# A decode-attention kernel: softmax maximum and values block one set sooner, the fifth key unit in halves, and the TensorE loop laid out afresh

## The chip, the cores and the metric

The kernel runs on one core of one Trainium2 chip. The metric is device time in microseconds (us), of which each kernel was run several times. "Span" is the time from the first to the last instruction in a profiled execution; it is about 2 us below the timed figure.

In the profile before, TensorE does the matrix work (9791 matmuls), VectorE (DVE in the profile, 1079 instructions) and ScalarE (ACT, 655) copy and do the softmax, SyncE (SP) issues 88 of the 91 transfers, and 16 DMA engines move the data.

## The reference, cut to what matters

One token is decoded. The work that counts is attention over a cache: 8 key/value heads, 65536 positions of 256 numbers each, in bf16, so 268 MB of keys and as much of values. 16 query heads share them, two per key/value head. Projections and a small gated MLP come on top.

```python
q = (x @ wq).reshape(B, Sq, Hq, Dh)...            # one token, 16 heads of 256
scores = jnp.einsum("bhqd,bhkd->bhqk", q, k) * (Dh ** -0.5)
p = _softmax(scores, axis=-1)
o = jnp.einsum("bhqk,bhkd->bhqd", p, v)
... @ wo                                           # plus the residual and the MLP
```

Every byte of the cache is used once. The whole kernel moves 549 MB.

## The kernel before: the parts that matter

Keys come in 32 units (k0, k1, ...) of 8 MB, 4 units to a head, and so do values (v0, v1, ...). There are three slots of 8 MB in on-chip memory: slots 0 and 1 alternate between key units, and slot 2 takes values. SyncE issues the transfers in one fixed order, and each issue waits until its slot is free:

```python
    def k_item(u):                       # key unit u goes into slot u % 2
        need = [("FREE", u - 2)] if u >= 2 else ()
        if 2 <= u < U:                   # U = 4: k2 and k3 in halves
            need = {0: [("FREEH", u - 2)], 1: need}
        slot_item("k", u, u % 2, [... two halves ...] if u < U else None, need)

    def v_item(t):                       # value unit t goes into slot 2
        slot_item("v", t, 2, None, [("VFREE", t - 1)] if t else [...])

    for u in range(U - 1): k_item(u)     # k0 k1 k2, all in halves
    v_item(0)
    k_item(U - 1); k_item(U); k_item(U + 1)          # k3 (halves), k4, k5
    for t in range(1, NT):               # v1 k6 v2 k7 ...
        v_item(t)
        if t + U + 1 < NU: k_item(t + U + 1)
```

TensorE goes through one key unit per turn, in 8 sets. A set transposes 16 positions per partition, multiplies them with the query (QK) and lays the scores out (JT). From turn 4 on, a turn also has a values block: unit v(t) is multiplied with the softmax weights in turn t + 4, since the maximum of a whole head (4 key units) is needed first. That maximum takes two small matmuls (M1T and BC) with VectorE work between, and every fourth turn ScalarE then takes the exponentials.

```python
    def turn_K(u):
        ...
        at = {(3, 0): ghostly(lambda: pe_m1t(...)), (4, 0): ghostly(lambda: pe_bc(...)),
              (SETS - 1, 0): ghostly(lambda: pe_oT(v))}     # (set, step): softmax matmuls
        k_sets(u, range(0, CSETS + 1), at)       # sets 0..4 (CSETS = 4)
        bar()                                    # the loop's code is cut into parts here
        ghostly(block)()                         # values block: 64 matmuls of 512 columns
        bar()
        k_sets(u, range(CSETS + 1, SETS), at)    # sets 5..7
```

The end of the block releases slot 2 (VFREE), half of the unit releases half of a key slot (FREEH), and the end of the turn releases all of it (FREE). In the first four turns the block is jumped over; `ghostly` marks what is left out there.

TensorE's instructions are one hardware loop over turns. Even and odd turns have their own code for the sets, as they read different slots, and share the block. In memory the order is: odd first part, even first part, block, odd second part, even second part. Turn 0 is an even one.

```python
   with eng.If_ne(parity, 0):  turn(... odd ...)
   with eng.If_eq(parity, 0):  turn(... even ...)
```

## Time and profile before

| | before |
|---|---|
| time, median of the first 3 runs | 1286.32 us (1285.24 to 1288.13) |
| span of the profiled execution | 1284.3 us |
| moved | 549 MB, 427 GB/s over the span |
| DMA queue, share of 16 engines | 99.2% |
| TensorE busy | 986.9 us (77%) |

From the page of the kernel before: the busy time of each engine, then rows of the picture in 40 slices (each about 32 us; a digit is a tenth), and the summary of the chain that ended last.

```profile
PE 986.9 (77%) x9791; PEld 660.5 (51%) x9791; DVE 576.1 (45%) x1079; ACT 436.1 (34%) x655; POOL 8.0 (1%) x38
...
DMA  9999899999999999999999999999999999999998
GB/s 405 412 432 438 339 443 425 425 447 433 427 429 449 429 425 447 431 429 425 449 433 425 431 447 429 425 447 433 427 425 451 431 425 435 443 429 425 411 449 354
...
DMA 65%; PE 24%; ACT 6%; issue 3%; SPq 2%; DVE 0%; ACTq 0%; DVEq 0%
```

The DMA engines are the busy ones. One slice alone stands out before the very end: the fifth, near 128 to 160 us, with 339 GB/s. The windows view of the same trace puts the stretch with the gap beside the steady part, and then looks into the gap (a packet counts in the window in which it starts, so shares over 1 are possible; PEclk is the granted clock of TensorE, 1.00 is full):

```profile
core 0: us, PE busy (x) PEld busy (x) DVE busy (x) ACT busy (x) POOL busy (x), PEclk, DMA share, GB/s
127.00:176.00 49.00, 41.85 (x430) 29.58 (x430) 27.30 (x53) 22.53 (x36) 0.00 (x0) 0.93 0.87 369
176.00:1182.00 1006.00, 787.94 (x7794) 532.60 (x7786) 461.71 (x861) 350.72 (x526) 0.00 (x0) 0.87 1.00 434
...
144.00:148.00 4.00, 3.60 (x38) 2.62 (x35) 2.68 (x6) 2.15 (x4) 0.00 (x0) 1.00 0.91 393
148.00:152.00 4.00, 2.20 (x36) 1.04 (x36) 0.69 (x2) 2.65 (x8) 0.00 (x0) 1.00 0.00 0
152.00:156.00 4.00, 4.00 (x55) 2.21 (x55) 1.11 (x3) 0.62 (x3) 0.00 (x0) 1.00 0.74 262
```

From 148 to 152 us no packet starts. What happens there is in the timeline (start, duration, engine, line, operation; in brackets the idle time before it and what ended it; "issue" there means that the profile shows nothing that it waited for). First TensorE in turns 0 and 4, then SyncE's issues of k5 and v1:

```profile
47.53 1.44 PE L411 MATMUL ps_t<-ident_f,ring 128*128 128x128 f32 x6 [6.56 <-issue]
...
130.50 1.97 PE L411 MATMUL ps_t<-ident_f,ring 128*128 128x128 f32 x8 [3.79 <-DMA ring<-in_A_k_cache_dram]
...
149.80 1.90 PE L411 MATMUL ps_o<-ring,p_sb 128*4 128x512 bf16 x32 [2.02 <-ACT p_sb L572]
151.63 0.61 PE L411 MATMUL ps_m<-rowsum,ones_f 128*128 128x2 f32 x4
152.17 1.90 PE L411 MATMUL ps_o<-ring,p_sb 128*4 128x512 bf16 x32
```

```profile
126.65 0.33 SPq L882 DMA_DIRECT2D ring<-in_A_k_cache_dram  x1
154.11 0.33 SPq L882 DMA_DIRECT2D ring<-in_A_v_cache_dram  x1
```

The view of the chain that ended last (start, duration, what) has k4 from its issue to its landing:

```profile
103.83 26.62 DMA ring<-in_A_k_cache_dram
```

Read the timeline from the bottom. v1 is issued at 154.11 us, as soon as the values block of turn 4 is done with v0. The transfer ahead of it, k5, landed at 150.63 (the landing times in this document are the completions of the semaphores in the trace). So the queue stood empty. The block was late because turn 4 began only at 130.50, when the whole of k4 had landed, though TensorE was free from 126.70. And k4, one transfer of 8 MB, was issued late because all of k2 had to be read first.

After that there is no gap of this kind. From 176 to 1202 us a unit lands every 19.35 us, 8.39 MB / 19.35 us = 434 GB/s. TensorE waits in nearly every turn, as the waits view of the whole execution says (who waited for whom: us in total, times, longest):

```profile
PE ps_t L411 <- DMA ring<-in_A_k_cache_dram: 136.5, 28, 6.5
PE ps_o L411 <- DMA ring<-in_A_v_cache_dram: 82.3, 26, 13.2
```

### The profile page before, as it was taken

What the parts mean: (1) busy time and instruction counts of PE and PEld (TensorE: products, weight loads), DVE (VectorE), ACT (ScalarE), POOL (GpSimd) and SP (SyncE); (2) the same over time, 40 slices, a digit from 0 to 9 for tenths busy, and PEclk for the clock granted to TensorE, in tenths of its full rate; (3) what the DMA queues carried; (4) which work ended last, traced back from release to release, by engine and by line L of the source; (5) the groups of instructions that cost most, each with busy time, mean ns of one, the idle gap of its engine ahead of it and who ended that gap; (6) DMA issues with size and microseconds to landing.
All of it is one profiled execution on the core that took longest, in us unless ns stands there. A gap on an engine that the chain in (4) does not pass through costs nothing.

```text
span 1284.3 us, 23619 instructions
## 1 busy us (share of the span) xinstructions
PE 986.9 (77%) x9791; PEld 660.5 (51%) x9791; DVE 576.1 (45%) x1079; ACT 436.1 (34%) x655; POOL 8.0 (1%) x38
## 2 busy tenths in 40 slices
PE   4799888787688777787886797687788778786573
PEld 3576565555455555454554465454455545554321
DVE  4476464444444443453543454443444543444210
ACT  1355443333333433333333243333433333332200
POOL 2000000000000000000000000000000000000000
PEclk9899898878988887897888888878988887998787
DMA  9999899999999999999999999999999999999998
GB/s 405 412 432 438 339 443 425 425 447 433 427 429 449 429 425 447 431 429 425 449 433 425 431 447 429 425 447 433 427 425 451 431 425 435 443 429 425 411 449 354
DMA packets 13444, 549.20 MB, mean 428 GB/s; under 512 B 1398, under 2 KB 3448, under 8 KB 4088
## 3 DMA queue, kind: packets, MB, share of 16 engines
q1 hardware_dynamic: 13426, 549.03, 99.2%
q8 instruction: 8, 0.13, 0.0%
q14 instruction: 4, 0.03, 0.0%
q10 hardware_dynamic: 6, 0.00, 0.0%
HBM read 549.03 MB, written 0.00 MB: 427 GB/s over the span
## 4 chain that ended last, share of the span: by engine, by line
DMA 65%; PE 24%; ACT 6%; issue 3%; SPq 2%; DVE 0%; ACTq 0%; DVEq 0%
DMA ring<-in_A_v_cache_dram 44%; DMA ring<-in_A_k_cache_dram 21%; PE ps_t L411 9%; PE ps_o L411 9%; ACT kt_all L481 5%; PE ps_q L411 4%; SPq L882 2%; PE ps_m L411 2%; DMA ring<-in_A_wo_dram 1%; ACT S_sb L562 1%; ACT p_sb L572 0%; DVE kt_all L479 0%; DVE kt_all L698 0%; ACTq L984 0%; PE ps_s L411 0%
## 5 line engine op out<-in xcount | busy, mean ns | idle before, releaser
L411 PE MATMUL ps_t<-ident_f,ring 128*128 128x128 f32 x4096 | 620.5, 296 | 167.4 <-DMA ring<-in_A_k_cache_dram 136.5
L479 DVE COPY kt_all<-ps_t 128x1024 bf16<-128x1024 bf16 x768 | 486.9, 684 | 401.4 <-PE ps_q L411 393.3
L411 PEld LDWEIGHTS ps_t<-ident_f,ring 128*128 128x128 f32 x4096 | 481.1, 150 | 330.4 <-issue 160.6
L481 ACT ACTIVATE kt_all<-ps_t 128x1024 bf16<-128x1024 bf16 x256 | 261.9, 1023 | 571.3 <-PE ps_q L411 571.2
L411 PE MATMUL ps_o<-ring,p_sb 128*4 128x512 bf16 x2044 | 160.6, 469 | 97.2 <-DMA ring<-in_A_v_cache_dram 82.3
L411 PE MATMUL ps_q<-kt_all,q_cur 128*2 128x512 bf16 x2056 | 172.6, 414 | 0.7 <-DVE kt_all L479 0.6
L503 ACT ACTIVATE s<-ps_q 98x512 bf16<-98x512 f32 x257 | 151.6, 590 | 1.3 <-PE ps_q L411 1.3
L411 PEld LDWEIGHTS ps_o<-ring,p_sb 128*4 128x4 bf16 x2044 | 50.5, 95 | 171.4 <-issue 120.7
L572 ACT ACTIVATE p_sb<-S_sb 128x128 bf16<-128x128 bf16 x64 | 18.9, 307 | 173.4 <-PE ps_o L411 173.1
L587 DVE RECIPROCAL rs<-ps_m 128x4 f32<-128x4 f32 x29 | 5.3, 182 | 148.1 <-PE ps_m L411 148.1
L411 PEld LDWEIGHTS ps_s<-sel_bf,s 128*128 128x128 bf16 x1032 | 65.0, 98 | 5.4 <-ACT s L503 1.9
L411 PE MATMUL ps_s<-sel_bf,s 128*128 128x8 bf16 x1032 | 63.7, 167 | 1.3 <-ACT s L503 1.3
L630 DVE CAST ob_sb<-ps_o 100x512 bf16<-100x512 f32 x29 | 20.1, 691 | 97.6 <-PE ps_o L411 97.6
L411 PEld LDWEIGHTS ps_q<-kt_all,q_cur 128*2 128x2 bf16 x2056 | 26.6, 79 | 49.0 <-issue 49.0
L411 PEld LDWEIGHTS ps_m<-rowsum,ones_f 128*128 128x128 f32 x116 | 18.8, 231 | 18.1 <-issue 18.1
L481 ACT ACT_TABLE_LOAD x7 | 9.0, 1283 | 50.7 <-PE ps_q L411 50.7
L411 PE MATMUL ps_m<-rowsum,ones_f 128*128 128x2 f32 x116 | 21.3, 288 | 0.0
L532 DVE TENSOR_REDUCE m1p<-S_sb (+1 forms) x33 | 13.9, 422 | 4.4
L411 PE MATMUL ps_q<-ring,oT_h 128*1 128x448 bf16 x28 | 8.1, 467 | 9.8 <-DMA ring<-in_A_wo_dram 9.8
L530 DVE CAST S_sb<-ps_s 128x256 f32 (+1 forms) x33 | 13.6, 413 | 1.9 <-PE ps_s L411 1.9
L562 ACT ACTIVATE S_sb<-S_sb,negmax 128x512 bf16<-128x512 bf16 x16 | 13.2, 850 | 3.0 <-DVE negmax L556 3.0
L411 PE MATMUL ps_m<-diag,ones_f 2*128 2x2 f32 x58 | 11.0, 256 | 0.6 <-DVE diag L547 0.6
(94 smaller groups left out, 134.0 us busy)
## 6 DMA issues: line engine op xcount, KB each, us to landing
ring<-in_A_k_cache_dram SPq DMA_DIRECT2D x8, 4096.0 KB, 30.4
ring<-in_A_v_cache_dram SPq DMA_DIRECT2D x1, 4096.0 KB, 28.1
ring<-in_A_wq_dram SPq DMA_DIRECT2D x1, 3584.0 KB, 11.8
ring<-in_A_wo_dram SPq DMA_DIRECT2D x7, 448.0 KB, 22.6
ring<-in_A_v_cache_dram SPq DMA_DIRECT2D x1, 2048.0 KB, 32.6
ring<-in_B_w_gate_dram SPq DMA_DIRECT2D x1, 1568.0 KB, 15.5
ring<-in_B_w_up_dram SPq DMA_DIRECT2D x1, 1568.0 KB, 18.9
ring<-in_B_w_down_dram SPq DMA_DIRECT2D x2, 784.0 KB, 21.6
```

The source lines that it names most:

```text
L411: return pe.matmul(*a, **k)
L479: O(e, ("EV", s, m), lambda it: nc.vector.tensor_copy(out=kt[:, :], in_=tb[:, :]), f"ev{m}")
L481: O(e, ("EV", s, m), lambda it: nc.scalar.activation(out=kt[:, :], in_=tb[:, :], func=ACTF.Copy), f"ev{m}")
L503: O("act", ("EVQ", s), lambda it: nc.scalar.activation(out=s2[s % 2][0:QROWS, :], in_=ps_q[0:QROWS, :], func=ACTF.Copy), "evq")
L530: O("dve", ("SCOPY", u), lambda it: nc.vector.tensor_copy(out=S_sb[:, at(it, SBN), :], in_=ps_sn), "sc")
L532: O("dve", ("SMAX", u), lambda it: nc.vector.tensor_reduce(out=m1p[:, :, at(it, 1)], in_=S_sb[:, at(it, SBN), :].rearrange("p n i -> p i n ...
L562: O("act", ("EXP", h, i), lambda it, i=i: nc.scalar.activation(out=S_sb[:, :, i], in_=S_sb[:, :, i], func=ACTF.Exp, bias=negmax[:, i:i + 1 ...
L572: O("act", ("PC", t, c), lambda it: nc.scalar.activation(out=p_sb[:, c, :, :], in_=S_sb[:, n:n + CH, :], func=ACTF.Copy), "pc")
L587: O("dve", ("RS", t), lambda it: nc.vector.reciprocal(out=rs[:, :, :], in_=ps_m[0:P, C_TOT:C_TOT + NH * rep]))
L630: O("dve", ("OB", t), lambda it: nc.vector.tensor_copy(out=ob_sb[0:OROWS, :], in_=ps_o[0:OROWS, :]))
L882: eng.dma_start(fn[0], fn[1]).then_inc(sems[sem], 16)
```

## The change

It has three parts. The fifth key unit, k4, is taken in halves like the first four, so its first half may be issued when half of k2 has been read. The values block moves from after set 4 to after set 3 of each turn, and the two softmax matmuls that come before it move with it. And the code of the even turn's second part comes right after the block, so turn 0, which jumps over the block, comes out right there.

```diff
@@ sizes
+    UH = U + 1
@@ k_item
-        if 2 <= u < U:
+        if 2 <= u < UH:
             need = {0: [("FREEH", u - 2)], 1: need}
-        slot_item("k", u, u % 2, [...halves...] if u < U else None, need)
+        slot_item("k", u, u % 2, [...halves...] if u < UH else None, need)
@@ k_sets (which load a set waits for)
-                W_item("pe", ... ("k", min(u, U - 2 + u % 2), 1))
+                W_item("pe", ... ("k", min(u, UH - 1 - (UH - 1 - u) % 2), 1))
@@ turn_K
-        at = {(3, 0): ghostly(lambda: pe_m1t(v + U - 1)), (4, 0): ghostly(lambda: pe_bc(v + U - 1)),
+        at = {(2, 2): ghostly(lambda: pe_m1t(v + U - 1)), (3, 0): ghostly(lambda: pe_bc(v + U - 1)),
-        k_sets(u, range(0, CSETS + 1), at)
+        k_sets(u, range(0, CSETS), at)
         ... values block ...
-        k_sets(u, range(CSETS + 1, SETS), at)
+        k_sets(u, range(CSETS, SETS), at)
@@ the loop's code (k counts its parts: 0 first sets, 2 second sets)
-                        with eng.If_ne(parity, 0): ... odd turn ...
-                        with eng.If_eq(parity, 0): ... even turn ...
+                        for odd in (1, 0) if k == 0 else (0, 1):
+                            if odd:
+                                with eng.If_ne(parity, 0): ... odd turn ...
+                            else:
+                                with eng.If_eq(parity, 0): ... even turn ...
```

The number of matmuls and the bytes moved are the same.

More of the change, by code (lines that the diff above doesn't have):

```diff
@@ L270, in k_item @@
         need = [("FREE", u - 2)] if u >= 2 else ()
-        if 2 <= u < U:
+        if 2 <= u < UH:
             need = {0: [("FREEH", u - 2)], 1: need}
-        slot_item("k", u, u % 2, [("slot%d" % (u % 2), CH), ("half%d" % (u % 2), CH)] if u < U else None, need)
+        slot_item("k", u, u % 2, [("slot%d" % (u % 2), CH), ("half%d" % (u % 2), CH)] if u < UH else None, need)
     def v_item(t):
@@ L727, in k_sets @@
             if q % CSETS == 0:
-                W_item("pe", ("k", u, 0) if q == 0 else ("k", min(u, U - 2 + u % 2), 1))
+                W_item("pe", ("k", u, 0) if q == 0 else ("k", min(u, UH - 1 - (UH - 1 - u) % 2), 1))
             s = u * SETS + q
@@ L1026, in loop @@
                             continue
-                        with eng.If_ne(parity, 0):
-                            turn(it, it, b0, b1, False)
-                            if k == len(cuts[0]) - 1:
-                                step_regs(("iter",))
-                        with eng.If_eq(parity, 0):
-                            turn(it, it, a0, a1, False)
+                        for odd in (1, 0) if k == 0 else (0, 1):
+                            if odd:
+                                with eng.If_ne(parity, 0):
+                                    turn(it, it, b0, b1, False)
+                                    if k == len(cuts[0]) - 1:
+                                        step_regs(("iter",))
+                            else:
+                                with eng.If_eq(parity, 0):
+                                    turn(it, it, a0, a1, False)
                     step_regs(("turn",))
```

## The prediction

> **What bounds the kernel now.** The transfers. The page shows the 16 DMA engines 90% busy or more in nearly every slice: 549 MB at 427 GB/s over 1284.3 us. From 176 us on, the chain of waits runs through DMA with TensorE pieces only between. By the landing times in the trace, from 176 to 1202 us an 8 MB unit lands every 19.35 us, each issued 13 us or more before the one ahead of it landed; the windows view gives 176 to 1182 us a DMA share of 1.00. There a sooner TensorE cannot help.

> The one hole is at the start: over 127 to 176 us the DMA share is 0.87, 369 GB/s. Unit k4 is issued at 103.83 us (release of unit 2) and lands at 130.45; TensorE stands from 126.65 to 130.50 for it, then restarts at half clock (eight transposes take 1.97 us, not 1.09). The first values block ends at 154.1, where v1 is issued. But k5 landed at 150.63. So v1 lands 25.28 us after k5 instead of 19.35, and k5 itself 20.18 after k4: lost 5.93 + 0.83 = 6.76 us.

> **What the change does there.**
> 1. k4 in halves: its first half is issued when half of unit 2 is read (about 92 us), and lands about 120.8. Turn 4 starts straight on, 3.85 us sooner and without the half-clock restart (its first set took about 2.5 us longer than the usual 2.85): v1 about 6.4 us sooner.
> 2. The values block one set sooner: another 2.9 us.
> 3. Loop layout: turn 0 stalls 6.56 + 1.27 us ("issue") at the jump to its second part, then runs at half clock; about 8 us can go, but turn 3 then waits for k3 (landing near 100.4), so perhaps 2 us reach turn 4. [...] five 16 KiB instruction packets between 20 and 52 us (one at 45.04, inside the stall), none again until 1210 us. So the gain comes once.

> v1 would be issued at about 143 to 145 us, some 5 us before k5 lands at about 149.8. An issue on an idle queue costs about 2.4 us (v1: 21.81 us from issue to landing), so the hole closes entirely, and everything later shifts with it. The parts overlap; each alone I estimate at about 6, 2.9 and below 1 us, capped at the 6.76 us hole. The softmax chain in fewer sets may cost TensorE about 1 us a turn; it waits 3 us for v there anyway.

> **Prediction.** 1286.32 - 6.8 = 1279.5 us; range 1278.0 to 1281.8. Faster by over 2%: 0.01; within 2%: 0.985; slower: 0.005.

> **In the profile:** DMA share 1.00 from k4's landing to v1's; v1 landing near 169 us, not 175.9; the 6.56 us stall in turn 0 gone; no wait for k4 at about 126 us; TensorE waiting longer for v (about 6 us a turn, not 3) and less for k in the steady turns, the 19.35 us rhythm unchanged.

> **What would make it wrong:** transfers pacing below 19.35 us per unit with earlier issue; a new hole where the split k4 or the tail's weight loads wait; a jump stall moved to another turn (the odd turn's second part now lies last); the end (1202 to 1284 us) not shifting along with the landings.

## The result, and the profile after

| | before | changed |
|---|---|---|
| time, median of 4 runs each | 1286.43 us | 1278.75 us (1277.88 to 1279.96) |
| ratio, 95% interval | | 0.994 (0.9923 to 0.9957) |
| span of the profiled execution | 1284.3 us | 1276.0 us |
| v1 issued / landed | 154.11 / 175.92 us | 144.31 / 168.25 us |
| from v1's landing to the last load's | 1105.91 us | 1105.11 us |

Ratios here and below are the mean time of one kernel's fast runs over that of the other's of the same rounds, so not quite the ratio of the medians that are quoted. The changed kernel was timed again later beside another run of the kernel before: 1279.65 against 1287.92 us, ratio 0.9936 (0.9922 to 0.995).

The page of the changed kernel, the same rows as before:

```profile
PE 976.1 (76%) x9791; PEld 638.2 (50%) x9791; DVE 570.2 (45%) x1079; ACT 436.6 (34%) x655; POOL 8.0 (1%) x38
...
DMA  9999999999999999999999999999999999999998
GB/s 405 430 428 440 437 431 436 431 429 440 433 429 438 427 440 433 431 438 427 436 436 431 438 429 431 438 431 431 438 427 438 436 431 438 427 436 438 409 434 360
...
DMA 76%; PE 19%; SPq 2%; ACT 1%; issue 1%; DVE 1%; ACTq 0%; DVEq 0%
```

The fifth slice is now 437 GB/s, and the chain is DMA for 76% of the span instead of 65%. The windows view of the changed kernel, for the same stretches:

```profile
127.00:176.00 49.00, 43.86 (x496) 30.00 (x495) 28.56 (x56) 24.02 (x39) 0.00 (x0) 1.00 1.01 438
176.00:1182.00 1006.00, 775.06 (x7739) 508.50 (x7741) 452.27 (x855) 347.44 (x520) 0.00 (x0) 0.88 1.00 433
...
148.00:152.00 4.00, 3.91 (x43) 2.70 (x42) 2.26 (x4) 1.90 (x3) 0.00 (x0) 1.00 1.02 442
```

The hole is closed, and the steady part has the same rate, 433 against 434 GB/s. Its timeline, TensorE, then SyncE, and v1 from its issue to its landing in the view of the chain:

```profile
41.20 0.26 PE L412 MATMUL ps_s<-sel_bf,s 128*128 128x8 bf16 x4 [0.98 <-issue]
...
100.46 1.97 PE L412 MATMUL ps_t<-ident_f,ring 128*128 128x128 f32 x8 [5.09 <-DMA ring<-in_A_k_cache_dram]
...
124.84 1.06 PE L412 MATMUL ps_t<-ident_f,ring 128*128 128x128 f32 x8 [0.18 <-ACT kt_all L482]
...
140.00 1.90 PE L412 MATMUL ps_o<-ring,p_sb 128*4 128x512 bf16 x32 [2.02 <-ACT p_sb L573]
141.83 0.61 PE L412 MATMUL ps_m<-rowsum,ones_f 128*128 128x2 f32 x4
142.36 1.90 PE L412 MATMUL ps_o<-ring,p_sb 128*4 128x512 bf16 x32
```

```profile
124.61 0.33 SPq L883 DMA_DIRECT2D ring<-in_A_k_cache_dram  x1
144.31 0.33 SPq L883 DMA_DIRECT2D ring<-in_A_v_cache_dram  x1
```

```profile
144.31 23.94 DMA ring<-in_A_v_cache_dram
```

The stall of 6.56 us in turn 0 is gone (0.98 us is left). Turn 3 now waits 5.09 us for k3, but turn 4 starts at 124.84 us without waiting for a load. v1 is issued at 144.31, and k5 landed at 148.89: 4.58 us of lead where there were 3.48 us of empty queue. In the waits view TensorE now waits longer for values and less for keys:

```profile
PE ps_o L412 <- DMA ring<-in_A_v_cache_dram: 191.3, 33, 12.2
PE ps_t L412 <- DMA ring<-in_A_k_cache_dram: 48.3, 20, 5.1
```

The sum grew, from 82.3 + 136.5 = 218.8 us to 191.3 + 48.3 = 239.6 us, and the kernel is faster all the same: in the steady turns the transfers set the time, so moving TensorE's wait about cost nothing and gave nothing (433 against 434 GB/s there).

### The profile page after: what moved, and what is told of

It is laid out like the page before. It is cut to its first block, busy times and chain, and to the rows that moved or that the text cites. A ratio compares the mean times of both kernels' runs of the same rounds, so it can differ in the third digit from the quotient of the medians.

```text
span 1276.0 us, 23620 instructions
## 1 busy us (share of the span) xinstructions
PE 976.1 (76%) x9791; PEld 638.2 (50%) x9791; DVE 570.2 (45%) x1079; ACT 436.6 (34%) x655; POOL 8.0 (1%) x38
## 4 chain that ended last, share of the span: by engine, by line
DMA 76%; PE 19%; SPq 2%; ACT 1%; issue 1%; DVE 1%; ACTq 0%; DVEq 0%
DMA ring<-in_A_v_cache_dram 70%; PE ps_o L412 13%; DMA ring<-in_A_k_cache_dram 5%; PE ps_t L412 3%; SPq L883 2%; PE ps_m L412 2%; PE ps_q L412 2%; ACT kt_all L482 1%; DMA ring<-in_A_wo_dram 1%; DVE kt_all L480 0%; ACT S_sb L563 0%; PE ps_s L412 0%; DVE kt_all L699 0%; DVE m1p L533 0%; DVE kt_all L835 0%
## 5 line engine op out<-in xcount | busy, mean ns | idle before, releaser
L412 PE MATMUL ps_t<-ident_f,ring 128*128 128x128 f32 x4096 | 590.0, 286 | 71.9 <-DMA ring<-in_A_k_cache_dram 48.3
L412 PEld LDWEIGHTS ps_t<-ident_f,ring 128*128 128x128 f32 x4096 | 453.9, 144 | 227.6 <-issue 139.8
L412 PE MATMUL ps_o<-ring,p_sb 128*4 128x512 bf16 x2044 | 186.9, 531 | 195.6 <-DMA ring<-in_A_v_cache_dram 191.3
L412 PEld LDWEIGHTS ps_o<-ring,p_sb 128*4 128x4 bf16 x2044 | 55.2, 105 | 289.5 <-issue 265.7
L412 PE MATMUL ps_q<-kt_all,q_cur 128*2 128x512 bf16 x2056 | 164.7, 397 | 0.6 <-DVE kt_all L480 0.6
L531 DVE CAST S_sb<-ps_s 128x256 f32 (+1 forms) x33 | 13.6, 414 | 1.9 <-PE ps_s L412 1.9
L412 PEld LDWEIGHTS ps_m<-diag,ones_f 2*128 2x128 f32 x58 | 8.5, 182 | 10.5 <-DVE diag L548 10.5
```

What stands on the lines that cost most here:

```text
L412: return pe.matmul(*a, **k)
L531: O("dve", ("SCOPY", u), lambda it: nc.vector.tensor_copy(out=S_sb[:, at(it, SBN), :], in_=ps_sn), "sc")
```

## The experiments

Three theories stood at the start:

- **Hole theory** (mine): the gain is the hole in the transfers at the start, closed once. Each part of the change pays by what it does for the time at which v1 (and k5) is issued.
- **Fetch rival**: the gain is the jump stall of turn 0, taken away by the new layout.
- **Every-turn rival**: the values block sooner frees slot 2 sooner in each of 28 turns, so the gain is spread over the run.

Edits are given against the changed kernel. In each run the result was correct. The medians of the runs that take the change apart (the others follow below):

| run | halves of k4 | block sooner | layout | median us | ratio to before (95%) | v1 issued / landed in its profile |
|---|---|---|---|---|---|---|
| before | | | | 1286.43 | | 154.11 / 175.92 |
| h_only | yes | | | 1282.01 | 0.9961 (0.9947 to 0.9974) | 147.43 / 169.31 |
| v_only | | yes | | 1286.41 | 0.9993 (0.9979 to 1.0008) | 152.16 / 174.06 |
| l_only | | | yes | 1285.60 | 0.999 (0.9977 to 1.0004) | 153.11 / 175.07 |
| no_h | | yes | yes | 1283.20 | 0.9972 (0.9959 to 0.9986) | 150.37 / 172.27 |
| no_v | yes | | yes | 1280.81 | 0.9949 (0.9936 to 0.9962) | 149.56 / 171.56 |
| no_l | yes | yes | | 1279.23 | 0.9935 (0.9922 to 0.9947) | 146.50 / 169.79 |
| after_again | yes | yes | yes | 1279.65 | 0.9936 (0.9922 to 0.995) | 145.32 / 168.93 |

The kernels before beside them had medians of 1287.11 us (the first three parts and no_h), 1286.52 (no_v, no_l) and 1287.92 (after_again), and these three groups ran on different chips, so compare ratios across rows rather than medians.

### Each part alone

h_only keeps the halves alone:

```diff
-        at = {(2, 2): ...m1t..., (3, 0): ...bc...        # block after set 3
+        at = {(3, 0): ...m1t..., (4, 0): ...bc...        # block after set 4, as before
-        k_sets(u, range(0, CSETS), at)                   # (and the sets after the block likewise)
+        k_sets(u, range(0, CSETS + 1), at)
-                        for odd in (1, 0) if k == 0 else (0, 1):
+                        for odd in (1, 0):               # layout as before
```

> Fifth key unit in halves alone. Hole theory (the gain is the closed DMA hole at 127 to 176 us, worth at most about 8 us): turn 4 starts without its wait for k4, v1 is issued near 147.7 us, 2 to 3 us before k5 lands, so most of the hole closes: about 1281 us, v1 landing near 170.5. Fetch rival (the gain is the jump stall taken out of turn 0): no gain, 1286.4. Every-turn rival (the values block sooner frees the v slot sooner in each of 28 turns): no gain, 1286.4.

Measured: 1282.01 us, ratio 0.9961, so about 5 us of the 7.7 that the whole change gave (ratio 0.994). In its profile turn 4 started without waiting and v1 was issued at 147.43 us, 1.62 us before k5 landed. This is the largest part, as the hole theory said; both rivals had no gain here and fall as the whole story.

v_only keeps the earlier block alone:

```diff
-    UH = U + 1
+    UH = U
-                        for odd in (1, 0) if k == 0 else (0, 1):
+                        for odd in (1, 0):
```

> Maximum and values block one set sooner alone. Hole theory: turn 4 still waits for k4 until 130.5; v1 is issued near 151.2 and lands near 173.0 instead of 175.9: 1283.5 us. Fetch rival: 1286.4. Every-turn rival: the whole gain, about 1279.

Measured: 1286.41 us, ratio 0.9993 (0.9979 to 1.0008). That is less than the 2.9 us that I expected; its interval reaches from 2.7 us faster to 1.0 slower. In its profile v1 was issued 1.95 us sooner than before, not 2.9. The timeline of v_only shows why in that execution:

```profile
129.75 1.97 PE L412 MATMUL ps_t<-ident_f,ring 128*128 128x128 f32 x8 [4.56 <-DMA ring<-in_A_k_cache_dram]
...
135.14 1.97 PE L412 MATMUL ps_t<-ident_f,ring 128*128 128x128 f32 x8 [0.48 <-ACT kt_all L482]
```

After the wait for k4, eight transposes took 1.97 us in the second set too, where the kernel before was back at about 1.1 us. The granted clock in the windows view was 0.50 from 132 to 136 us and 0.61 from 136 to 140; before, it was 0.55 and 1.00. So the half-rate stretch after the wait for k4 (3.79 us before, 4.56 here) lasted about 5 us before and about 9 here. What the half clock takes in this execution is of the size of the effect that I wanted to measure. In any case the every-turn rival, which had the whole gain here, is out.

l_only keeps the layout alone:

```diff
-    UH = U + 1
+    UH = U
-        at = {(2, 2): ...m1t..., (3, 0): ...bc...
+        at = {(3, 0): ...m1t..., (4, 0): ...bc...
-        k_sets(u, range(0, CSETS), at)                   # (and the sets after the block likewise)
+        k_sets(u, range(0, CSETS + 1), at)
```

> Loop layout alone. Hole theory: turn 0 ends 8.5 us sooner (at about 49.7), but turn 4 still starts when k4 has landed (129.5, since the second half of k2 lands 1 us sooner), v1 is issued near 153.1: gain 1 to 2 us, about 1285. Fetch rival: the whole gain, about 1279. Every-turn rival: 1286.4.

Measured: 1285.60 us, ratio 0.999 (0.9977 to 1.0004). Turn 0 ended at 48.64 us instead of 58.16, so TensorE gained 9.5 us there, and the kernel gained about 1 by the ratio, which is not clear of zero. The fetch rival is out. The profile shows the 9.5 us dying mostly in two waits: turn 2 ended at 94.30 us, but k3's first half landed only at 100.39 (so turn 3 ended at 124.33, 2.3 us sooner than before), and then turn 4 waited for k4, which landed at 129.45.

### The whole change without one part

no_h is the changed kernel with `UH = U`; no_v has the block after set 4; no_l has the old layout. Each is one of the edits shown above.

> The whole change without the halves of the fifth key unit. Hole theory: turn 4 starts at 129.5 when k4 has landed, v1 is issued near 150.2 and lands near 172, against 168.25 with the halves: about 1282.3 us. Fetch rival and every-turn rival: the halves don't matter, about 1278.8.

> The whole change with the maximum and values block left where it was. Hole theory: v1 is issued near 147.2 us, 1.7 us before k5 lands at 148.9; a lead under about 2.4 us leaves a rest of the hole of about 1 us: about 1279.7 us, v1 landing near 169.2. Every-turn rival: no gain left, about 1286. Fetch rival: 1278.8.

> The whole change with the loop laid out as before. Hole theory: v1 is issued near 145, 5 us before k5 lands, so the hole itself closes; but the second half of k2 is issued only 3.4 us before the half ahead of it lands and loses 1 us again (landing 72.35 instead of 71.35): about 1280 us. Fetch rival: no gain, 1286.4. Every-turn rival: 1278.8.

The 2.4 us in the second of these is the estimate of the prediction, from v1 of the kernel before: 21.81 - 19.35 us.

Measured: without the halves 0.9972, which leaves less than half of the gain; v1 landed at 172.27, as expected within 0.3 us. Without the earlier block 0.9949: some 1.7 us of the gain are missing by the ratios against after_again (0.0013 of 1286), but the two intervals overlap. What is clear of noise, barely, is v_later below, with the block two sets later. The profiled run of no_v fell among its slowest, with v1 issued at 149.56 rather than the 147.2 expected. Without the new layout 0.9935: nothing is missing. So the layout, for all that it takes 7.0 us off turn 0 here (it ended at 56.67 us in no_l, at 49.66 with the layout), adds nothing that the runs can resolve once the other two parts are there.

What held up no_v's profiled v1, and made no_l's 1.5 us later than I had expected, is again the clock, this time after the softmax: in no_v it was 0.63 from 144 to 148 us. The first half of turn 4's values block in no_l:

```profile
140.55 3.54 PE L412 MATMUL ps_o<-ring,p_sb 128*4 128x512 bf16 x32 [2.02 <-ACT p_sb L573]
```

The same 32 matmuls took 1.90 us in the changed kernel's profile after the same wait of 2.02 us. The granted clock was 0.58 from 140 to 144 us in no_l and 1.00 in the changed kernel.

### Does the values block matter in every turn?

v_later moves the block the other way, to after set 5:

```diff
-        at = {(2, 2): ...m1t..., (3, 0): ...bc...
+        at = {(3, 0): ...m1t..., (4, 0): ...bc...
-        k_sets(u, range(0, CSETS), at)
+        k_sets(u, range(0, CSETS + 2), at)
         ... values block ...
-        k_sets(u, range(CSETS, SETS), at)
+        k_sets(u, range(CSETS + 2, SETS), at)
```

> The whole change, but the maximum and values block one set later than in the kernel before (two later than in the change). Hole theory: v1 is issued near 150.0 us, on an idle queue, and lands near 171.8 instead of 168.25; every later turn keeps its rhythm of 38.7 us, so the loss comes once: about 1282.3 us. Every-turn rival: the loss comes in each of 28 turns at about 0.27 us a set, 1294.

Measured: 1282.37 us, ratio 0.9963 (0.9951 to 0.9975). In the waits view of v_later the steady waits turned over completely:

```profile
PE ps_t L412 <- DMA ring<-in_A_k_cache_dram: 229.4, 28, 9.3
PE ps_o L412 <- DMA ring<-in_A_v_cache_dram: 29.2, 13, 13.8
```

TensorE now waits 229 us for keys and 29 for values, where the changed kernel had 48 and 191, though the kernels' times differ by about 3 us only. The steady rhythm did not move: from v1's landing to the last load took 1105.71 us, against 1105.11 in the changed kernel and 1105.91 before. The whole loss is v1's: landed at 171.44 instead of 168.25. That is the once-only loss of the hole theory; the every-turn rival had 1294. It also shows that the place of the block counts: 0.9951 to 0.9975 here against 0.9922 to 0.995 for after_again.

### Is anything left at the start?

h_plus takes the sixth key unit in halves too (`UH = U + 2`).

> The whole change with the sixth key unit in halves too. Hole theory: its first half would be issued near 112 us instead of 124.6, but 124.6 is already 4.9 us before k4 lands and there is no hole left at the start: the same as the change, 1278.8 within 0.7 us. If early issue still paid something at the start, it would be faster by 1 us or more.

> The changed kernel unaltered, for its time on the same chip as the run beside it: 1278.8 us, v1 landing near 168.3.

Measured on the same chip: 1279.11 us (0.993) and 1279.65 us (0.9936). Their intervals overlap almost wholly. In the profile of h_plus the first half of k5 was issued at 112.85 us, 12 us sooner than k5 in the changed kernel, and nothing came of it. This profile also shows that the start is not always free of a hole: half clock fell into the values block (the granted clock was 0.62 from 140 to 144 us and 0.53 from 144 to 148, and its two halves took 2.35 and 3.58 us instead of 1.90 each), v1 was issued only 2.4 us before k5 landed, and it landed at 171.00 us, 2.8 us late. No version that I ran beats the changed kernel clear of noise.

### How early is early enough? Runs with a delay put in

The kernel before lost another 1.09 us: the second half of k2, issued at 58.16 us, 3.40 us before the half ahead of it landed, took 10.80 us from landing to landing instead of 9.71. In the changed kernel it took 9.71. I wanted to know whether its late issue or the jump's instruction fetch did this. Three kernels put n transposes of the identity, results unused, before turn 0:

```diff
         W("pe", "PSQ_ZERO")
         W("pe", "PSO_ZERO")
+        O("pe", "DELAY", lambda it: [mm(ps_tf[0][:, ...], lhsT=ident_f[:, :], rhs=ident_f[:, :],
+                                        is_transpose=True, start=True, stop=True) for i in range(n)][-1])
```

> The whole change, and 90 transposes of the identity (about 12 us of TensorE, results unused) put in before turn 0, so that turn 0 ends near 58.2 us as it did with the jump stall, but without the jump. If the 1 us that the second half of k2 lost before came from its late issue (3.4 us ahead), it is lost again here: landing near 72.4 and about 1279.8 us. If it came from the jump's instruction fetch itself, the landing stays at 71.35 and the time at 1278.8.

> The whole change with 20 transposes of the identity before turn 0. The run with 90 delayed turn 0 by 14.5 us (12.7 of transposes and a stall of 5.7 at the loop's entry), more than planned; 20 should start it near 28.2 us, some 4.6 us late. Hole theory: turn 2 then ends near 99.9 us, still before k3's first half lands at 100.4, so the delay dies in that wait: k5 and v1 issued as in the change, no hole, 1279.3 us within 0.8. If each us of TensorE at the start counted: 1283.5.

> The same with 45 transposes: turn 0 starts near 32 us and ends near 58.1 us, as late as in the kernel before, but without its jump stall. Hole theory: the second half of k2 is issued about 3.5 us before the half ahead of it lands and loses about 1 us (landing near 72.4), turn 2 ends near 103.7, k5 and v1 are issued about 4 us ahead: v1 lands near 170.3, about 1280.7 us. If the 1 us at k2 came from the jump's fetch itself, k2 lands at 71.35.

None of the three set up the state that I wanted, and each for a reason worth knowing. With n = 90 the transposes took 12.7 us, and then TensorE stalled for another 5.71 us at the loop's entry before turn 0 could start, at 38.11 us. With n = 20 they nearly fitted into the time in which TensorE waits for k0 anyway (turn 0 started at 23.98 us instead of 23.59); k2's second half was issued at 48.32 us, as early as without a delay, so this run is just the changed kernel once more (1279.57 us, 0.9945). With n = 45 the second half of k2 was issued at 52.91 us, only 3.3 us late, but the stall came back at another place, between turns 0 and 1:

```profile
58.82 1.94 PE L412 MATMUL ps_t<-ident_f,ring 128*128 128x128 f32 x8 [5.87 <-issue]
```

so that turn 2 ended at 106.65 us instead of 95.31 and turn 3 at 129.44 instead of 124.61 (1283.63 us, 0.9972). With n = 90 turn 3 ended at 135.43 us and the kernel took 1289.11 us (1.0013): the whole gain of the change was lost. Turn 3 ended 10.8 us later than in the changed kernel and v1 landed 12.0 us later (180.23 us). So a late TensorE at the start is paid for about in full once the leads are used up.

The misses still help with the question, put together with all other runs. Here is each transfer at the start that was issued less than about 6 us ahead: its lead (landing of the transfer ahead minus its own issue; negative means an empty queue) and its loss (time from landing to landing, less 19.35 us for a unit or 9.71 for a half).

| lead us | loss us | where |
|---|---|---|
| 5.2 to 4.9 | 0.0 in each | k2's second half in v_only and no_l; k5 in l_only, no_h, v_later, changed; v1 in delay_20 |
| 4.6 to 4.2 | 0.0, 0.1, 0.0, 0.3, 0.3 | v1 in changed; k5 in v_only; v1 in after_again; k5 in no_l and no_v |
| 4.0, 4.1 | 0.6, 1.5 | k5 in after_again and delay_20 |
| 3.8, 3.4 | 0.8, 1.1 | k5 and k2's second half in before |
| 2.6, 2.6, 2.4, 1.6 | 1.3, 1.8, 2.8, 0.9 | v1 in no_l, delay_45, h_plus, h_only |
| 0.9, 0.6, 0.5 | 1.6, 2.3, 3.2 | k2 (first half) in delay, k5 in delay_45, k2 (second half) in delay |
| -0.35, -0.4, -0.9, -0.9 | 3.1, 3.0, 3.5, 3.5 | v1 in v_later and no_v; k5 and v1 in delay |
| -1.5, -3.0, -3.5, -4.3 | 4.0, 5.5, 5.9, 6.9 | v1 in no_h, v_only, before, l_only |

At a lead of about 4.5 us and more next to nothing is lost. Below that the loss grows, unevenly, to about 2.6 us at zero, and from there on each us of empty queue costs one us more. k2's second half fits this curve at 3.40 us of lead. And it lost nothing in v_only and no_l, which have the old layout and stalls of 4.25 and 2.58 us, and of 3.83 and 2.49 us, in turn 0 (the block's jump and the parts lie elsewhere), but issued it 5.2 and 4.9 us ahead. The packets in the trace of before show the loss itself: 16 of the queue's packets were under way at 59.3 us, only 10 at 60.0, and 16 again from 62.0 us on, where the changed kernel had 16 throughout; no instruction packet of 16 KiB fell into that time (the nearest ended at 53.2 us). So it was the queue that ran dry, as a short lead would have it; what I did not get is a run with that lead and no jump.

Why 4.5 and not the time of a start? The 16 engines do not finish a transfer together. In the kernel before, 16 packets of k5 were under way until 148.34 us, 9 at 148.7 and 1 from 149.43, while k5 landed at 150.63: the first engine ran dry 2.3 us before the landing. The first packets of v1 on the engines started 0.95 to 1.65 us after its issue. Together that is 2.3 + 1.65 = 3.95 us, an estimate from these two figures; it comes near the 4.5 us and does not explain all of it. Nor is the 2.3 us simply the time of one packet, though a packet of 64 KB takes 2.42 us: with the packets of 32 KB of k2's halves, 1.21 us each, the first engine ran dry 2.1 us before the landing as well (59.48 and 61.56 us). What sets this spread is open.

## Why the prediction was right, point by point

- **What bounds the kernel**: right. Every run kept 19.35 us a unit and about 1106 us from v1's landing to the last load (1104.8 to 1107.0 over all profiles), whatever TensorE did meanwhile. One detail was misread: the issues there are 11.8 us and more ahead, not 13, which changes nothing at a need of 4.5.
- **The hole as the only thing to win, 6.76 us**: right in kind, a little small. v1 landed 7.67 us sooner: 6.76 of the hole, plus 1.00 from the second half of k2 (1.09 us lost before, which I saw only in the landing times and did not count), less 0.09 of scatter in the earlier landings. The span fell by 8.3 us: these 7.67, another 0.48 us that v3 had lost in the profiled execution of before although it was issued 13.6 us ahead, and some tenths from the end. What cost v3 that time is open.
- **v1 issued at 143 to 145 us, k5 landing near 149.8**: measured 144.31 and 148.89.
- **"5 us is enough"**: right by luck, with the wrong threshold. I took 2.4 us, the cost of an issue on an idle queue (v1: 21.81 - 19.35 = 2.46 us). The runs put the lead that loses nothing at about 4.5 us. The changed kernel's 4.58 and 4.27 us in its two profiles just have it; the margin that I thought was 2.6 us hardly exists, and half clock after the softmax, which the prediction did not think of, would use it up (lead 2.6 us in no_l, 2.4 in h_plus). That v1 lost nothing at all is shown for these two executions of the changed kernel only; k5 lost 0.6 us in one of them.
- **The parts alone, 6, 2.9 and below 1 us, capped together**: measured by the ratios 5.0, 0.9 and 1.3 us, the last two not clear of zero. The halves lead and the layout is small, as said. The block's part alone was over-estimated: in the profiled execution a longer stretch of half clock after k4's wait (about 9 us instead of 5) took part of it. Beside the halves (no_l against h_only: 0.9935 against 0.9961, from two different rounds of runs) it gave 3.3 us.
- **The layout: 8 us of TensorE, of which 2 reach turn 4**: right for the layout alone: in l_only turn 0 ended 9.5 us sooner and turn 3 2.3 us sooner. With the whole change turn 0 ended 8.5 us sooner and turn 3 2.0 us sooner (124.61 against 126.65); of the 6.5 us between, 5.09 died in the wait for k3 and the rest in the half clock after it (a granted clock of 0.50 from 97.39 to 104.22 us). Of these 2.0 us the layout's own share is small: no_l ended turn 3 at 125.16. Both traces have five instruction packets of 16 KiB in the first 53 us and no other of that size before 1205 us, though the loop jumps in each of 32 turns. That fetching them is what stalls the jump was my reading; no run showed it.
- **TensorE waiting about 6 us a turn for v instead of 3, less for k**: right, 191.3 / 28 = 6.8 us, and 1.7 instead of 4.9 for k.

## What to carry to other kernels

When the transfers are gap-free in the steady part, look for the time in the landings of the first few: list when each was issued and when the one ahead of it landed, and treat a short lead as a loss even though the queue never stands empty; with transfers of 4 and 8 MB, short meant under about 4.5 us. A change that freed a buffer sooner paid once here, where the queue ran dry (v1 landed 7.67 us sooner), and next to nothing in the loop that was transfer-bound already (1105.11 against 1105.91 us). And a stall on another engine, however plain in the timeline, was worth only what survived the next wait for data: 8.5 us of TensorE came to 2, and to nothing that the runs can resolve beside the other two parts.
